# An attention and Fourier-mixing kernel: identity first, block products for every chunk, GpSimd's loads reordered

## Chip, cores and metric

The kernel runs on one core of one Trainium2 chip. Its time is the device time of one execution in microseconds (us); the clock that the throttle granted to TensorE was 1.000 of full speed in the profiled execution.

## What is computed

The input has 4 batches, 8 heads, 768 positions and 64 channels a head. Attention sees the last 96 positions and the first 8 (global) ones, with a bias that falls with the distance at a slope of its own for each head. Its output, 768 x 512 a batch, is mixed by a Fourier transform along both axes (real part), added to itself, normalized, and sent through a two-layer perceptron.

```
scores = q @ k.T / 8 - slope[h] * dist ; outside the band and the first 8 keys: -1e9
x = softmax(scores) @ v                      # heads side by side: (4, 768, 512)
u = x + real(fft(fft(x, axis=1), axis=2))
un = (u - mean(u)) / sqrt(var(u) + 1e-6)
out = u + relu(un @ w_ch1) @ w_ch2           # 512 -> 2048 -> 512
```

## The kernel before

**Units and lists.** All work is cut into units. TensorE's units have a letter and a number: A is attention, M is mixing, H is the first layer of the perceptron and G the second one. A small operation on another engine is named after the unit that created it (A1.0, H9.0) or is T.n if it belongs to no unit of TensorE. The table `ORDER` holds, for each of the five engines (TensorE PE, ScalarE ACT, VectorE DVE, GpSimd POOL, SyncE SP), the list of names in the order in which this engine issues them. Each engine runs its list in order; which engine makes a small operation follows from the list in which its name stands. The numbers of the class `Plan` (`LAT`, `SLOW`, costs in `later`) are a model of the chip; they decide in which of several free PSUM banks a unit works, and in which order the program is emitted, while the order on each engine comes from the lists.

**Attention.** For batches 0 and 1 q and k are loaded by GpSimd's queue (T.11 to T.14, T.19, T.20 for batch 0; T.28 to T.33 for batch 1), with a cast to float16 on the way, all but the first pair of heads: that pair comes by SyncE's and ScalarE's queues (reads T.0, T.2, T.4, T.6, casts T.1, T.3, T.5, T.7). TensorE turns q and k with the identity matrix (`trans`: A0, A1, A5, A6, A15 in batch 0, A25, A26, A30, A34 in batch 1), the turned pair is copied out of PSUM, and the keys of the inner tiles are copied once more into `kB` (the key swap, line 685). A score unit (A2 to A4 and so on) adds the distance bias on TensorE, with the scaled identity and the distance table `dist` (T.9), and ScalarE takes the exponential. The `av` units multiply by v; VectorE divides the result (line 836) into X. v is loaded by T.15 to T.18, T.21 to T.24 (batch 0) and T.58 to T.61 (batch 1), and its inner tiles are copied into `vB` (T.66 to T.69, T.85 to T.88). Batches 2 and 3 are turned by DMA on SP's queue and use the distance table `dist_k` (T.35) by a multiplication instead.

**Mixing.** X is folded (VectorE f1 to f4, g1, g2: T.70 to T.83 for batch 0, T.93 to T.98 for batch 1; partly M0 and M1 on TensorE). The y units (M2, M3, M9, M10 in batch 0; M15, M16, M18, M19 in batch 1) multiply by the table t1 (T.26), the u units (M7, M8, M13, M17) by t2 (T.27); M4 to M6 spread X by a permutation (T.25). For batches 1 to 3 X goes to memory and comes back in rows (T.91 reads it for batch 1). Each batch has three chunks of 256 rows, 12 in all. M11, M12 and M14 turn the normalized chunks 0 to 2, later ones are turned by DMA.

**Perceptron.** H units 8c to 8c+7 make the hidden layer of chunk c. They need the weight pieces of `w_ch1` (T.54 to T.57); unit H(8c+j) needs piece j/2. The second layer has two forms. For chunks below `CS` (0 and 1) `pg_unit` makes it plainly: two halves of 128 rows, each of four units of four matmuls of 512 columns (line 1372), so G0 to G15. Other chunks use block products (`s_sums`, `pg_units`): the product of 2 x 2 blocks is made by 7 products of blocks instead of 8, each of eight matmuls of 256 columns (line 1486), in five units a chunk, six in the last. They need four sums of blocks of the hidden layer (s1 to s4, lines 1450 to 1463, 128 x 1024 each) and four blocks of sums of the weights (`w2_sums`, T.259 to T.262), of which one is written over a part of `w_ch2` itself, so that the last plain product has to be through (`pgdone`). The pieces of `w_ch2` are loaded by T.62 to T.65.

What a unit of GpSimd's load queue waits for is also the eighth load before it, as at most eight are under way:

```
if p[9]:
    t = max(t, (self.lanes[p[9] - 1] if p[9] > 0 else self.soft[-p[9] - 1])[0])
```

Of the kernel before, what the change touches and what calls it, by code (L numbers as in the profile page):

```python
# [14 lines left out]
P = 128  # L15


class Ring(str):

    k = 0  # L20
# [4 lines left out]
class Plan:  # L25
# [11 lines left out]
    LAT = {"ACT": 0.14, "DVE": 0.12, "POOL": 0.08}  # L37
# [84 lines left out]
    def op_go(self, eng, name, start):  # L122
# [6 lines left out]
        if eng == "POOL":  # L129
            self.ports.append((start, end, 1 if dma else 0 if outs and outs[0][0] in ("vB", "kB") else 2))  # L130
# [21 lines left out]

    SHARED = {"kB": 1, "vB": 1, "sid": 1, "f1": 0, "f2": 0, "f3": 0, "z": 0, "g0": 0, "w": 0, "s": 0, "w2a": 0, "w2t": 0, "ex": 0}
# [3 lines left out]
    def beside(self, start, cost, kind):  # L157

        left, t = cost, start
        names = self.todo["POOL"]  # L160
        ports = self.ports[-3:]
        if names:
            s = self.op_start("POOL", names[-1])
            if s is not None:
                p = self.made[names[-1]]
                ports = ports + [(max(s, start), max(s, start) + p[0]["POOL"][0], 1 if p[7] else 0 if p[3] and p[3][0][0] in ("vB", "kB") else 2)]
        for a, b, dma in ports:
            if b <= t:
                continue
            if a > t:  # L170
                if a - t >= left:
                    break
                left -= a - t
                t = a
            rate = self.SLOW[kind][dma]
            if (b - t) * rate >= left:
                return t + left / rate - start
            left -= (b - t) * rate
            t = b
        return t + left - start  # L180
# [40 lines left out]
    def unit_start(self, unit):  # L221
# [7 lines left out]
        if not there:  # L229
# [22 lines left out]
        ),  # L252
        "ACT": (
# [9 lines left out]
        ),  # L263
        "DVE": (
# [11 lines left out]
        ),  # L276
        "POOL": (
# [5 lines left out]
        ),  # L283
        "SP": (
            "T.6 T.0 T.9 T.136 T.35 T.127 T.133 T.128 G7.1 T.134 T.91 G3.1 T.10 T.137 T.130 T.100 T.131 T.101 T.102 T.176 T.182 T.177 T.34 T.185 T.183 "
            "T.140 T.205 T.212 T.206 T.186 T.211 T.149 T.179 T.180 T.150 T.151 T.229 T.189 T.228 T.223 T.222 T.198 T.199 T.200 T.240 T.239 T.245 T.246 "
            "T.256 T.258 T.257 "
# [56 lines left out]
def act(n):  # L344
    return 0.1 + n / 1180.0


def dve(n):
    return 0.13 + n / 960.0
# [6 lines left out]
def pool(n):  # L356
    return 0.16 + n / 1080.0


@with_exitstack  # L360
def kernel(
# [25 lines left out]
    CS = 2  # L387
# [132 lines left out]
    def load_v(b, hp):  # L520
# [7 lines left out]
        if b == 1:  # L528
            for t in range(2 - hp % 2 * 2):
# [3 lines left out]
                swq(four, 1.08, [], [("v", b, hp, t), ("v", b, hp + 1, t)], (1536, 0.93))  # L533
# [172 lines left out]
    def score(b, hp, g):  # L706
# [3 lines left out]
        def run(start, ring):  # L710
# [37 lines left out]
            e = pl.pe((0.45, 0.45, 0.34)[g] if pem else 0.24, start, "64x64" if pem else "64x32")  # L748
# [61 lines left out]
    def av(b, hp):  # L810
# [28 lines left out]
        def part(start, ring, x, k):  # L839
# [15 lines left out]
            pl.later([("DVE", 0.17 + 0.03 * m + m * dve(384), lambda: norm(po, k))], free(*XT[b]), e,  # L855
# [10 lines left out]
    def bounce(b):  # L866
# [26 lines left out]
        pl.later([("POOL", 1.1, rg)], xw + [("xr", b), ("c", "back")], 0.0, [("xg", b)], dma=(128, 4.94), rank=0)  # L893

    def fold_s(b):
# [3 lines left out]
        for n, (c0, cw) in enumerate(parts):  # L899
# [43 lines left out]
            pl.later([("DVE", (4 if b else 2) * dve2(cw), f3)], [("f2", b, n)], 0.0, [("f3", b, n)])  # L943
# [844 lines left out]
```

## Time and profile before

| | |
|---|---|
| median of 3 runs | 248.52 us (247.92 to 248.96) |
| profiled execution | 248.1 us |
| its span, first to last instruction | 246.3 us |
| TensorE busy | 230.6 us (94%) |
| VectorE, ScalarE, GpSimd busy | 193.6, 138.6, 114.1 us |
| read from memory, written | 31.48 MB, 8.65 MB |

Busy times are unions of instruction times on an engine; a matmul's time includes its way through the pipeline, so the price of one in a row of many is the distance of the starts. The two views used most are the timeline (start, length, engine, line, operation, tiles, how many, and in brackets the idle time ahead of it and what ended it) and the stretches (for each stretch its length, then busy time and count of TensorE, its weight loads, VectorE, ScalarE, GpSimd, the granted clock, the share of DMA and GB/s).

### The profile page before, as it was taken

The page shows a single profiled execution, that of the slowest core. Times are in us where ns is not written, and L with a number is a line of the kernel's source. Part 1 is how long each engine was busy: PE and PEld are TensorE (multiplying, and loading weights), DVE is VectorE, ACT ScalarE, POOL GpSimd, SP SyncE. Part 2 cuts the span into 40 slices and gives each one's busy share as a digit, 9 for nine tenths or more (in the row PEclk, how much of TensorE's full clock was granted, in tenths as well). Part 3 has the DMA queues.
Part 4 walks back from the last instruction along what each step waited for, and adds up shares of the span by engine and source line. Part 5 has one row for each costly group of instructions (what it writes and reads, how often), then busy time and mean ns, then how long its engine had stood idle before and what let it go on. Part 6 is the DMA issues. An engine that isn't in the chain of part 4 may idle for free.

```text
span 246.3 us, 7605 instructions
## 1 busy us (share of the span) xinstructions
PE 230.6 (94%) x3251; PEld 191.2 (78%) x3251; DVE 193.6 (79%) x420; ACT 138.6 (56%) x226; POOL 114.1 (46%) x162
## 2 busy tenths in 40 slices
PE   7497896999999998999999999999999999999994
PEld 2375774788668567888988888898889898888883
DVE  2389995879974669999999699899998756746483
ACT  2289687874747458677447788464443761434200
POOL 8699985978391018999139046700210230011020
PEclk9999999999999999999999999999999999999999
DMA  7999999999999999999999989221380240040212
GB/s 178 171 163 141 157 223 148 201 189 201 125 133 168 211 181 204 111 139 114 220 208 266 136 110 148 50 23 22 133 296 4 43 130 0 0 130 1 89 65 106
DMA packets 96082, 32.89 MB, mean 134 GB/s; under 512 B 84304, under 2 KB 92624, under 8 KB 96048
## 3 DMA queue, kind: packets, MB, share of 16 engines
q0 software_dynamic: 66176, 17.06, 72.7%
q1 hardware_dynamic: 26560, 12.56, 25.8%
q10 hardware_dynamic: 3312, 2.79, 3.9%
q8 instruction: 25, 0.41, 0.7%
q14 instruction: 9, 0.07, 0.1%
HBM read 31.48 MB, written 8.65 MB: 163 GB/s over the span
## 4 chain that ended last, share of the span: by engine, by line
PE 49%; DMA 21%; DVE 15%; ACT 4%; POOL 4%; SPq 3%; issue 2%; ACTq 0%; DVEq 0%; POOLq 0%
PE ph L1341 21%; PE pgD L1486 12%; PE pgA L1486 9%; DMA v<-in_v_dram 6%; DMA t<-t1m 4%; DMA ident<-idm 3%; SPq L633 3%; DMA out_dram<-u 3%; PE pav L824 2%; ACT ex L768 2%; DMA unT<-un 2%; POOL qk L554 2%; DMA xr<-xd 2%; DVE tt L836 2%; DMA qk<-in_q_dram 2%
## 5 line engine op out<-in xcount | busy, mean ns | idle before, releaser
L1341 PE MATMUL ph<-unT,w 128*128 128x256 f16 x768 | 94.4, 273 | 1.4 <-DMA unT<-un 0.7
L1341 PEld LDWEIGHTS <-w 128*128 128x128 f16 x768 | 73.7, 98 | 13.2 <-issue 1.2
L1346 ACT ACTIVATE hT<-ph 128x512 f16<-128x512 f32 x73 | 42.9, 596 | 55.1 <-PE ph L1341 53.1
L1486 PEld LDWEIGHTS <-hT 128*128 128x128 f16 x320 | 31.0, 98 | 4.3 <-issue 0.4
L1287 POOL TENSOR_SCALAR sm<-sm 128x2 f32<-128x2 f32 x12 | 3.5, 291 | 58.7 <-ACT un L1280 58.3
L765 ACT ACTIVATE er<-sc 128x1024 f16<-128x1024 f32 (+1 forms) x24 | 22.3, 951 | 11.6 <-PE sc L739 8.0
L1347 DVE TENSOR_SCALAR hT<-ph 128x512 f16<-128x512 f32 x23 | 15.7, 687 | 12.6 <-PE ph L1341 12.6
L768 ACT ACTIVATE ex<-sc 128x1024 f16<-128x1024 f32 (+1 forms) x24 | 21.6, 955 | 5.7 <-PE sc L745 5.6
L1504 DVE SCALAR_TENSOR_TENSOR u<-pgA,sm,u 128x256 f32<-128x256 f32 (+1 forms) x30 | 16.9, 568 | 5.6 <-PE pgA L1486 5.1
L1504 DVE SCALAR_TENSOR_TENSOR u<-pgD,sm,u 128x512 f32<-128x512 f32 (+1 forms) x21 | 15.1, 720 | 3.2 <-PE pgD L1486 3.0
L1357 POOL DMA_INDIRECT out_dram<-u,back x4 | 4.6, 1146 | 27.8 <-DVE rev L1142 16.3
L889 POOL DMA_INDIRECT xr<-xd,back x3 | 4.6, 1525 | 26.1 <-PE sc L739 16.6
L1120 ACT ACTIVATE zy<-py 128x1024 f16<-128x1024 f32 (+1 forms) x13 | 11.1, 857 | 8.8 <-PE py L1107 6.1
L1372 PE MATMUL pg<-w,hT 128*128 128x512 f16 x64 | 16.0, 380 | 0.0
L780 DVE TENSOR_TENSOR ex<-er,mk 128x1024 f16<-128x1024 f16 (+1 forms) x24 | 15.1, 645 | 0.7 <-ACT er L765 0.7
L1280 ACT ACTIVATE un<-un 128x512 f16<-128x512 f16 x24 | 15.0, 625 | 1.1 <-DMA unT<-un 1.1
L1271 ACT ACTIVATE un<-u,sm 128x512 f16<-128x512 f32 x19 | 13.1, 717 | 2.4 <-DVE sm L1238 1.0
L554 POOL DMA_DIRECT2D qk<-in_k_dram x16 | 13.7, 901 | 1.1 <-DMA w<-in_moe_w_ch_dram 0.7
L824 PEld LDWEIGHTS <-ex 128*128 128x128 f16 x352 | 12.6, 97 | 2.0 <-issue 1.2
L824 PE MATMUL pav<-v,ex 128*128 128x65 f16 x224 | 13.1, 193 | 0.6 <-DVE x L836 0.5
L554 POOL DMA_DIRECT2D qk<-in_q_dram x16 | 13.6, 868 | 0.0
L836 DVE TENSOR_TENSOR x<-pav,rc 128x384 f16<-128x384 f32 x24 | 12.6, 554 | 0.6
(168 smaller groups left out, 489.3 us busy)
## 6 DMA issues: line engine op xcount, KB each, us to landing
w<-in_moe_w_ch_dram POOLq DMA_DIRECT2D x8, 512.0 KB, 13.5
out_dram<-u SPq DMA_DIRECT2D x15, 256.0 KB, 2.4
v<-in_v_dram POOLq DMA_DIRECT2D x12, 192.0 KB, 7.6
qk<-in_k_dram POOLq DMA_DIRECT2D x16, 96.0 KB, 6.8
qk<-in_q_dram POOLq DMA_DIRECT2D x16, 96.0 KB, 5.3
xr<-xd SPq DMA_DIRECT2D x3, 512.0 KB, 4.7
xd<-x ACTq DMA_DIRECT2D x2, 768.0 KB, 5.6
v<-in_v_dram POOLq DMA_DIRECT2D x8, 96.0 KB, 5.4
```

The lines of the kernel that those rows point to most:

```text
L554: nc.gpsimd.dma_start(qk16[n][:, w, :, h], src[b, h0 + h].rearrange("(i m) d -> m i d", m=P))
L765: A(mine(), cut(pa), AF.Exp, 0.0, 0.125)
L768: A(cut(expst[hp][:, :, g * 512:g * 512 + (384 if g == 2 else 512)]), cut(pa), AF.Exp, 0.0, 0.125)
L780: VT(o, mine(), m, op=ALU.mult)
L824: nc.tensor.matmul(o[:, s * 65:(s + 1) * 65], lhsT, w, start=(a == 0), stop=(a == len(ops) - 1), skip_group_check=True)
L836: VT(X[b][:, 3 * (k.start + h):3 * (k.start + h) + 3, 2 * hp * Dh:(2 * hp + 2) * Dh].rearrange("p y (h d) -> p y h d", d=Dh), pv[:, h, :, ...
L1341: nc.tensor.matmul(ph[:, a * CH:(a + 1) * CH].rearrange("p (x m) -> p x m", x=2), W1[0][:, d, jb * P:(jb + 1) * P], UNT[c][:, :, d, :], st ...
L1346: pl.later([("ACT", act(512), lambda: A(dst, ph, AF.Relu)), ("DVE", dve(512), lambda: V.tensor_scalar_max(dst, ph, 0.0))], [], e, [("h", c ...
L1347: ("DVE", dve(512), lambda: V.tensor_scalar_max(dst, ph, 0.0))],
L1372: nc.tensor.matmul(pg, HT[c][:, jb, t * P:(t + 1) * P], W2[0][:, jb, :], start=(jb == 0), stop=(jb == NJ - 1))
L1486: nc.tensor.matmul(o, lhs(j), rhs(j), start=(first and j == 0), stop=(j == NK - 1), skip_group_check=True)
L1504: V.scalar_tensor_tensor(o, x, r(t), acc, op0=ALU.mult, op1=ALU.add)
```

## The change

It has three parts, and the lists of all engines are written anew around them.

1. ScalarE's queue issues the identity (T.8) first, then its two reads of q and k (T.2, T.4), then the distance table (T.9, before on SP's queue), and after two casts `dist_k` (T.35, before on SP's queue). ScalarE now casts both parts of k, VectorE both parts of q.
2. `CS` is 0: chunks 0 and 1 also use block products. The G units are numbered anew: chunk c has G5c to G5c+4, the last G55 to G60. The block sums of chunk 0 are T.201 to T.204, of chunk 11 T.263 to T.266, the sums of weights T.270 to T.273. They wait no longer for plain products, and X of batch 1 lies in X's own buffer and not in that of the first loads. A block sum of chunk 3 and later may be made by GpSimd, and 13 of the 48 sums stand on GpSimd's list.
3. GpSimd's loads come in another order. In particular q and k of the fourth pair of heads come second, and t1 (T.26) comes behind t2 (T.27), two loads of v of batch 1 and a piece of `w_ch1`, and ahead of a piece of `w_ch2` (T.65).

Beside that some costs of the model are changed. Of the key swaps of batches 0 and 1 four move from GpSimd to VectorE (A1.0, A15.0, A6.0, A30.0) and one the other way (A5.0).

```diff
-    LAT = {"ACT": 0.14, "DVE": 0.12, "POOL": 0.08}
+    LAT = {"ACT": 0.18, "DVE": 0.12, "POOL": 0.08}
...
         "PE": (
-            "A0 A1 A5 A3 A4 A2 A8 A9 A15 A10 A11 A7 A6 A20 A18 A19 A14 A13 A12 A16 A30 A21 A17 A22 A23 A24 A37 A36 M0 A34 A25 M1 A35 M4 A28 A38 A26 M5 M2 "
-            "A39 A29 M3 M9 A32 M7 A33 A40 M8 M10 A31 M6 A27 M11 M13 A44 H2 H7 A43 H4 H3 M12 A42 H0 H1 A41 H12 G4 H13 H11 G0 H6 H5 M14 G1 G5 G6 H15 G7 H14 "
+            "A0 A1 A5 A4 A3 A15 A2 A20 A19 A18 A9 A8 A7 A6 A10 A11 A16 A12 A13 A14 A17 A30 A21 A22 A23 A24 A25 M1 A34 A26 M0 A36 A35 A38 A40 M4 A29 A28 "
+            "A39 M5 M2 M3 M9 A32 M7 A33 M8 A37 M10 M6 A27 A44 M11 A43 M13 A31 H1 H4 A42 A41 H2 H0 M12 H3 H5 H7 H13 H6 H15 H10 H9 H14 M19 M15 H11 G0 H12 "
+            "M14 M18 H8 M16 G1 G2 M17 G3 G4 G5 H16 H19 G6 A47 H17 G7 A46 H23 H21 G9 H20 A53 A51 H18 H22 G8 A55 A45 G10 H24 A54 A56 H30 G11 A50 A52 H27 "
...
+            "H64 G39 G40 H74 H78 G41 H72 H79 G42 H75 H73 G43 H76 G44 H77 H85 M32 H84 G45 H80 H82 G46 H86 H81 G47 H87 G49 H83 G48 G50 H90 H94 G51 H95 H92 "
+            "G52 H93 H88 G54 H91 H89 G53 G55 G56 G57 G58 G59 G60 "
...
         "ACT": (
-            "T.2 T.4 T.8 T.3 T.5 A1.2 A3.0 A4.0 A2.0 A8.0 A9.0 A7.0 A20.0 A18.0 A19.0 A13.0 A12.0 A14.0 A30.1 A37.0 A36.0 T.72 M0.0 T.77 M0.1 A25.1 M1.0 "
+            "T.8 T.2 T.4 T.9 T.5 T.7 T.35 A1.1 A3.0 A5.1 A2.0 A4.0 A20.0 A19.0 A9.0 A8.0 A7.0 A18.0 A12.0 A13.0 A14.0 A25.1 T.77 M1.0 M1.1 A26.1 M0.0 "
...
         "DVE": (
-            "T.7 T.1 T.49 T.51 A1.1 A5.1 A5.0 T.52 T.66 T.50 A15.1 A11.0 A10.0 A6.1 T.70 T.53 T.68 T.71 A16.0 T.69 A17.0 A22.0 A21.0 T.75 T.73 T.76 A23.0 "
+            "T.49 T.50 T.1 T.3 T.52 A1.2 T.51 A1.0 A15.1 A15.0 T.66 T.53 T.68 A6.1 A6.0 A11.0 A10.0 T.70 A16.0 A30.1 A17.0 A23.0 A24.0 T.75 T.71 T.76 "
...
+            "T.85 M13.2 A42.0 A41.0 T.93 T.94 T.95 T.96 T.201 T.97 T.272 T.98 T.270 T.273 T.271 G0.0 T.202 T.204 G1.0 G2.0 T.203 G3.0 G4.0 T.207 M17.0 "
...
         "POOL": (
-            "T.12 T.11 T.20 T.15 T.16 T.19 T.13 T.14 T.36 T.22 A1.0 T.21 T.18 T.17 T.30 T.31 T.23 A15.0 T.24 T.33 A6.0 T.28 T.67 T.32 T.29 A30.0 T.25 "
-            "T.65 T.26 T.27 T.61 T.60 T.59 A34.0 A25.0 T.56 T.57 T.55 T.58 T.54 T.111 A26.0 T.88 T.118 T.62 T.84 T.64 T.87 T.63 T.121 T.86 M7.8 T.119 "
+            "T.11 T.12 T.19 T.20 T.14 T.15 T.16 T.18 T.13 T.17 T.21 T.22 T.36 T.31 T.30 A5.0 T.24 T.23 T.28 T.29 T.25 T.32 T.33 T.67 T.69 T.27 T.61 T.55 "
+            "T.60 T.26 T.65 T.54 A25.0 T.59 A34.0 T.56 T.58 A26.0 T.62 T.87 T.118 T.84 T.106 T.88 T.111 T.57 T.86 T.116 T.63 T.104 T.64 T.105 T.120 T.108 "
...
+            "T.173 M20.5 T.228 T.148 T.235 T.236 T.238 T.241 T.190 M23.11 M26.5 T.197 T.243 T.246 M29.5 T.245 T.249 T.252 T.254 M29.11 T.259 M32.5 T.266 "
+            "T.262 "
...
         "SP": (
-            "T.6 T.0 T.9 T.136 T.35 T.127 T.133 T.128 G7.1 T.134 T.91 G3.1 T.10 T.137 T.130 T.100 T.131 T.101 T.102 T.176 T.182 T.177 T.34 T.185 T.183 "
+            "T.6 T.0 T.10 T.91 T.130 T.127 T.136 T.133 T.128 T.131 T.137 T.206 T.205 T.134 T.100 T.101 T.185 T.176 T.34 T.186 T.177 T.102 T.216 T.217 "
...
-    CS = 2
+    CS = 0
...
+        def slow(fn):
+            return [("POOL", pool2(NK * P), lambda: fn(nc.gpsimd))] if c > 2 else []
...
-        pl.later([("DVE", us, s1)], hs + sfree(0), 0.0, [("s", c, 1)], rank=1)
+        pl.later([("DVE", us, s1)] + slow(s1), hs + sfree(0), 0.0, [("s", c, 1)], rank=1)
...
-        pl.later(ways if soon else ways[:1], needs, 0.0, [tok], lat=1.0 if soon else 3.2, dma=us)
+        pl.later(ways if soon or tok == ("dk",) else ways[:1], needs, 0.0, [tok], lat=1.0 if soon else 3.2, dma=us)
```

More of the change, by code (lines that the diff above doesn't have):

```diff
@@ L129, in op_go @@
         if eng == "POOL":
-            self.ports.append((start, end, 1 if dma else 0 if outs and outs[0][0] in ("vB", "kB") else 2))
+            self.ports.append((start, end, 1 if dma else 0 if outs and outs[0][0] in ("vB", "kB", "ts", "w1s", "s") else 2))
         if dma:
@@ L165, in beside @@
                 p = self.made[names[-1]]
-                ports = ports + [(max(s, start), max(s, start) + p[0]["POOL"][0], 1 if p[7] else 0 if p[3] and p[3][0][0] in ("vB", "kB") else 2)]
+                ports = ports + [(max(s, start), max(s, start) + p[0]["POOL"][0], 1 if p[7] else 0 if p[3] and p[3][0][0] in ("vB", "kB", "ts", "w1s", "s") else 2)]
         for a, b, dma in ports:
@@ L854, in part @@
             m = k.stop - k.start
-            pl.later([("DVE", 0.17 + 0.03 * m + m * dve(384), lambda: norm(po, k))], free(*XT[b]), e,
+            pl.later([("DVE", 0.08 + 0.03 * m + m * dve(384), lambda: norm(po, k))], free(*XT[b]), e,
                      [("x", b, hp, z) for z in range(k.start, k.stop)], CD(b, ring), ring=ring, rank=RA(b))
@@ L892, in bounce @@
         pl.later([("SP", 0.38, rd)], xw + free("xr", b), 0.0, [("xr", b)], lat=2.0, dma=(128, 10.4))
-        pl.later([("POOL", 1.1, rg)], xw + [("xr", b), ("c", "back")], 0.0, [("xg", b)], dma=(128, 4.94), rank=0)
+        pl.later([("POOL", 1.6, rg)], xw + [("xr", b), ("c", "back")], 0.0, [("xg", b)], dma=(128, 4.94), rank=0)
     def fold_s(b):
@@ L942, in fold_s @@
             pl.later([("DVE", 2 * dve2(2 * cw) + 0.6 * (b + n == 0), f2)], [("f1", b, n)] + free("ww", IW(b, n)), 0.0, [("f2", b, n)])
-            pl.later([("DVE", (4 if b else 2) * dve2(cw), f3)], [("f2", b, n)], 0.0, [("f3", b, n)])
+            pl.later([("DVE", (3.45 if b else 2) * dve2(cw), f3)], [("f2", b, n)], 0.0, [("f3", b, n)])
             if b == 0:
@@ L1144, in r0 @@
             Y[(b, 0, 3, "r")], Y[(b, 3, 3, "r")] = rev[:, 0], rev[:, 1]
-        pl.later([("POOL", 0.8, lambda: r0(nc.gpsimd.tensor_copy)), ("DVE", 0.3, lambda: r0(V.tensor_copy))], [("y", b, 0, 3), ("y", b, 3, 3)] + free("rev0", b), 0.0,
+        pl.later([("POOL", 1.1, lambda: r0(nc.gpsimd.tensor_copy)), ("DVE", 0.3, lambda: r0(V.tensor_copy))], [("y", b, 0, 3), ("y", b, 3, 3)] + free("rev0", b), 0.0,
                  [("y", b, 0, 3, "r"), ("y", b, 3, 3, "r")], [("free", "zy", 2 * b + 1)])
@@ L1274, in centre @@
         for a in range(2):
-            pl.later([("ACT", 0.62, lambda a=a: un("ACT", a)), ("DVE", 1.3 if c < 2 else 0.38, lambda a=a: un("DVE", a))],
+            pl.later([("ACT", 0.62, lambda a=a: un("ACT", a)), ("DVE", 1.3 if c < 2 else 0.55, lambda a=a: un("DVE", a))],
                      [("u", c, a)] + free("un", c), 0.0, [("un", c, a)])
@@ L1288, in rstd @@
             nc.gpsimd.tensor_tensor(r, r, mhalf, op=ALU.pow)
-        pl.later([("POOL", 0.82, rstd)], [("ss", c, 0), ("ss", c, 1)], 0.0, [("rstd", c)], rank=2)
+        pl.later([("POOL", 1.25, rstd)], [("ss", c, 0), ("ss", c, 1)], 0.0, [("rstd", c)], rank=2)
     def nt_dma(c):
@@ L1359, in st @@
                                          in_=UT[c].rearrange("p r d -> p (r d)"), in_offset=None)
-        pl.later([("POOL", 1.1, st)], needs, 0.0, [], [("free", "u", c + pl.U0)] * 2, dma=(128, 11.25), rank=0)
+        pl.later([("POOL", 1.25, st)], needs, 0.0, [], [("free", "u", c + pl.U0)] * 2, dma=(128, 11.25), rank=0)
     def pg_unit(c, t, part):
@@ L1447, in new, with s1, s3, s2 @@
             return SX[c, i]
-        def s1():
-            VT(new(0), block(1, 0), block(1, 1), op=ALU.add)
-        def s3():
-            VT(block(1, 0), block(0, 0), block(1, 0), op=ALU.subtract)
-        def s2():
-            VT(new(1), SX[c, 0], block(0, 0), op=ALU.subtract)
-        def s4():
+        def s1(on=V):
+            on.tensor_tensor(new(0), block(1, 0), block(1, 1), op=ALU.add)
+        def s3(on=V):
+            on.tensor_tensor(block(1, 0), block(0, 0), block(1, 0), op=ALU.subtract)
+        def s2(on=V):
+            on.tensor_tensor(new(1), SX[c, 0], block(0, 0), op=ALU.subtract)
+        def s4(on=V):
             if lean:
                 SX[c, 2] = SX[c, 1]
-                VT(SX[c, 2], block(0, 1), SX[c, 1], op=ALU.subtract)
+                on.tensor_tensor(SX[c, 2], block(0, 1), SX[c, 1], op=ALU.subtract)
             else:
-                VT(new(2), block(0, 1), SX[c, 1], op=ALU.subtract)
+                on.tensor_tensor(new(2), block(0, 1), SX[c, 1], op=ALU.subtract)
         us = dve2(NK * P)
+        def slow(fn):
+            return [("POOL", pool2(NK * P), lambda: fn(nc.gpsimd))] if c > 2 else []
         def sfree(i):
@@ L1471, in s_sums @@
         k = 3 * (c - LATE)
[L1472 to L1475 removed]
+        pl.later([("DVE", us, s1)] + slow(s1), hs + sfree(0), 0.0, [("s", c, 1)], rank=1)
+        pl.later([("DVE", us, s2)] + slow(s2), [("s", c, 1)] + sfree(1), 0.0, [("s", c, 2)], [] if lean else [("free", "sx", k)], rank=1)
+        pl.later([("DVE", us, s4)] + slow(s4), [("s", c, 2)] + ([("p6", c)] if lean else sfree(2)), 0.0, [("s", c, 4)], [] if lean else [("free", "sx", k + 1)], rank=1)
+        pl.later([("DVE", us, s3)] + slow(s3), [("s", c, 1)], 0.0, [("s", c, 3)], rank=1)
     def pg_units(c):
```

26 lines of the change are left out of this document (13 added, 13 removed), and 49 rows, old and new, of the table ORDER.

## The prediction

> **What bounds the kernel now.** I read the page first (shares, slices), then three stretches, then TensorE's waits, then single stretches of the timeline.
>
> ```profile
> PE 230.6 (94%) x3251; PEld 191.2 (78%) x3251; DVE 193.6 (79%) x420; ACT 138.6 (56%) x226; POOL 114.1 (46%) x162
> PE   7497896999999998999999999999999999999994
> DMA  7999999999999999999999989221380240040212
> ```
> ```profile
> 0.00:43.00 43.00, 32.92 (x737) 24.35 (x737) 29.55 (x74) 27.98 (x36) 35.25 (x56) 1.00 1.76 169
> 43.00:60.00 17.00, 16.36 (x357) 13.98 (x355) 14.62 (x37) 11.61 (x18) 15.09 (x25) 1.00 1.43 198
> 60.00:243.00 183.00, 181.30 (x2162) 152.89 (x2160) 149.21 (x310) 98.98 (x172) 63.78 (x82) 1.00 0.84 120
> ```
> The first number behind the comma is PE's busy time. From 60 to 243 us PE stands idle for 1.7 of 183 us, so there the time is the sum of the matmuls, whatever VectorE or GpSimd do. Of the 12.4 us that PE is idle up to 243, 10.1 lie before 43 us. There DMA is full, and PE waits for it and for small steps:
> ```profile
> PE pt L654 <- DMA ident<-idm: 2.3, 1, 2.3
> PE sc L745 <- POOL mk L686: 1.8, 2, 1.1
> PE py L1107 <- issue: 1.5, 1, 1.5
> PE pz L1645 <- DVE eg L1640: 1.4, 1, 1.4
> PE py L1107 <- DMA t<-t1m: 0.8, 1, 0.8
> PE ph L1341 <- DMA w<-in_moe_w_ch_dram: 0.6, 1, 0.6
> ```
> So a change pays by fewer matmuls, or by less waiting before 60 us. The sum is made against the profiled run: 248.1 us, of which the span is 246.3; the median of the runs is 248.52, 0.4 above, which I add at the end.
>
> **Products of chunks 0 and 1.** They are 16 groups of four 512-column matmuls; they become 14 products of eight 256-column ones.
> ```profile
> 60.01 1.03 PE L1372 MATMUL pg<-w,hT 128*128 128x512 f16 x4
> 60.88 1.91 PE L1341 MATMUL ph<-unT,w 128*128 128x256 f16 x16
> ```
> ```profile
> 144.74 0.87 PE pgA L1486 x8
> 145.61 0.67 PE pav L824 x22
> ```
> The distance between starts is the price, as matmuls overlap: 0.87 us for a group of four, and 0.87 us for eight of 256 columns. So 16 x 0.87 = 13.9 becomes 14 x 0.87 = 12.2: **-1.7 us**, in a stretch where PE is the bound. It brings eight block sums of about 0.7 us and larger additions to VectorE, but 13 sums of chunks 3 to 11 go to GpSimd; VectorE has 34 idle us of 183 after 60 us, so this costs nothing in sum.
>
> **The 13 sums on GpSimd.** No such operation is in the trace. A GpSimd copy of 512 columns takes 0.63 us and one of 128 takes 0.32 (below), so 1024 columns with one input are about 1.0 us, and with two at most twice that if each input costs alike; I take 2.0, the upper end, as two operands are read, and 0 as the price on PE. In the new order each sum has PE work between its source and its user: for chunk 9's first sum H85, M32, H84, G45, H80, H82, about 5.2 us at 0.87 each; for the last chunk's s3, four products, 3.5 us. Cover is gone only if a sum takes over 3.5 us. What GpSimd's sums do to VectorE is seen here:
> ```profile
> 18.97 0.35 DVE L968 TENSOR_TENSOR eA<-x 128x384 f16<-128x384 f16 x1
> 19.23 1.21 DVE L969 TENSOR_TENSOR eA<-x 128x384 f16<-128x384 f16 x1
> ```
> ```profile
> 19.59 0.63 POOL L685 COPY mk<-qkT 128x512 f16<-128x512 f16 x1
> 20.28 0.32 POOL L686 COPY mk<-qkT 128x128 f16<-128x128 f16 x1
> ```
> An addition and a subtraction of the same size on VectorE take 0.35 and 1.21 us; the second lies beside GpSimd's copies and loses 0.9 us. If 13 x 2.0 us on GpSimd slow half of what VectorE does beside them, that is 13 us of VectorE, of the 34 that it has idle. The Trainium skill (SBUF — State Buffer, "Who interferes with whom") says that a VectorE operation with two SBUF inputs and a GpSimd operation that reads SBUF exclude each other for the whole instruction. By that rule the row of 1.21 us is one that stood still, and the trace agrees. As an estimate by it, 13 sums hold VectorE for up to 26 us instead of 13; that still fits into the 34, so the sum stays, and the rest of it is rival 4.
>
> **The start.** The identity is now first on ScalarE's queue, the distance table and dist_k last.
> ```profile
> 1.26 0.53 ACTq L570 DMA_DIRECT2D u<-in_k_dram  x1
> 1.82 0.51 ACTq L1610 DMA_DIRECT2D ident<-idm  x1
> 7.18 0.52 ACT L599 ACTIVATE hT<-u 128x384 f16<-128x384 f32 x1 [2.59 <-DMA u<-in_k_dram]
> 8.68 1.31 PE L654 MATMUL pt<-ident,hT 128*64 128x128 f16 x24 [2.32 <-DMA ident<-idm]
> ```
> PE's first transposes could have begun at 7.7 us, behind the cast of k, but the identity came at 8.6. Now that cast is the last; k is issued 0.5 us later, and no longer shares the first queue time with the distance table, which goes the other way by about as much. So PE starts at 7.3 to 8.3, I take 7.8: 0.9 us earlier. The key swap moves from GpSimd to VectorE, behind one more identity scaling: no gain there. But 0.9 us at 8 us is worth something only if nothing later on the way is later, and here one thing is.
>
> **GpSimd's loads.** The table t1 comes from GpSimd's queue behind other loads, and the first y product (M2) needs it.
> ```profile
> 24.29 1.03 POOL L585 DMA_DIRECT2D tt<-in_k_dram  x1
> 27.09 0.74 POOL L1678 DMA_DIRECT2D w<-in_moe_w_ch_dram  x1
> 28.38 0.57 POOL L1634 DMA_DIRECT2D t<-t2m  x1
> 28.92 2.93 POOL L531 DMA_DIRECT2D v<-in_v_dram  x3
> ```
> ```profile
> tt<-in_k_dram POOLq DMA_DIRECT2D x1, 384.0 KB, 6.3
> w<-in_moe_w_ch_dram POOLq DMA_DIRECT2D x1, 512.0 KB, 8.8
> t<-t2m POOLq DMA_DIRECT2D x1, 384.0 KB, 11.6
> v<-in_v_dram POOLq DMA_DIRECT2D x1, 192.0 KB, 12.3
> ```
> ```profile
> 27.83 10.04 DMA t<-t1m
> ```
> ```profile
> 38.01 1.03 PE L1107 MATMUL py<-t,ww 128*128 128x256 f16 x8 [0.78 <-DMA t<-t1m]
> 51.40 1.92 PE L1341 MATMUL ph<-unT,w 128*128 128x256 f16 x16 [0.57 <-DMA w<-in_moe_w_ch_dram]
> ```
> Issue plus time to landing: the last load of q and k (T.29) lands at 30.6, the permutation and a weight piece at 35.9, t1 at 37.9, t2 at 40.0, the first v at 41.2. Each comes out in order, so the queue is full: a step is 5.3, 2.0, 2.1, 1.3 us. In the new order t1 stands behind the same loads of q and k, the permutation and one weight piece, but also behind t2 (2.1) and two v loads (1.3 each): 4.7 us later. Against it, four key swaps (0.95 us each) leave this stretch of GpSimd and one comes in, and what copies are left stand behind the loads of q and k, so the queue is fed earlier: 0 to 2.9 us. The table dist_k, 160 KB, is added early at about 0.9 us (t1's 384 KB in 2.0). So t1 lands between 40.6 and 43.5 if the permutation and a weight piece take 5.3 us again, and between 38.7 and 41.6 if they go at t1's rate (656 KB in 3.4). I take 40.8, a little to the early side, since GpSimd no longer stops for a copy before these loads. VectorE and ScalarE allow M2 at about 39 to 40 by the order of their lists, so the table is the last.
> PE then starts M2 at 40.9 instead of 38.0, but with more done: three scores are moved ahead of M2 and one behind it, 1.0 us. From M2 to the first H unit it was 13.4 us, 2.1 of it waiting (1.5 issue, 0.6 weights); the waits mostly go, since M3 and M9 follow at once; the work is 11.3 less three scores, plus one, plus A43: about 10.95. So H1 starts at 51.85 with A43 (0.65 us) done besides: **-0.2 us** (from -2.3 to +2.5 by the ends for t1).
>
> **Behind it.** On SP's queue the read of batch 1's fold rows (T.91) moves ahead of the transposes of batch 2.
> ```profile
> SPq L633 <- DMA qk<-in_q_dram: 70.6, 3, 54.2
> ```
> Those wait for their loads for 54 us as it is, so a read that is due at about 60 us costs them nothing; were batch 1's attention later than these loads, they would wait for it. H6 and H7 need the weight piece T.57, now issued behind three loads of batch 2; A42 needs a value copy of GpSimd behind it: +0.3. G1 needs the weight sums, which were not needed before chunk 2.
> ```profile
> 61.52 0.96 DVE L909 TENSOR_TENSOR eA<-tt 128x1536 f16<-128x1536 f16 x1
> 71.20 0.74 DVE L1383 SCALAR_TENSOR_TENSOR u<-pg,sm,u 128x512 f32<-128x512 f32 x1
> ```
> ```profile
> L1427 DVE TENSOR_TENSOR tt<-w 128x1024 f16<-128x1024 f16 x2 | 1.5, 729 | 0.1
> ```
> On VectorE stand between A41 and G1: its division (1.3), the fold (61.5 to 71.2 less two strangers of 0.8: 8.9), one block sum (0.7), eight weight sums (8 x 0.7 = 5.6), 16.5 us. On PE 14 H units (12.2), G0, M12, M14 and four y units stand there, about 17. A tie: +0.5 (0 to 2.5). Queued behind the waiting G1 on PE is everything, as PE runs in order.
> The later waits:
> ```profile
> 96.67 1.91 PE L1341 MATMUL ph<-unT,w 128*128 128x256 f16 x16 [0.65 <-DMA unT<-un]
> ```
> Batch 1's fold starts some 3 us earlier, so this one should shrink: -0.3 (-1 to +1).
>
> Sum: -1.7 - 0.2 + 0.3 + 0.5 - 0.3 = -1.4, so 246.7, and on the scale of the median **247.1 us**. Its own range is 245.9 to 248.3.
>
> **Rivals.** (1) *The table t1 is later still, and the weights with it*: t1 at 42.7 (1.9 later) and T.57 0.8 later: 249.8. For it: DMA is full from 2 us on, so putting 0.77 MB ahead is paid unless the feed had gaps. Against: GpSimd has an idle gap and four copies less. It decides from t1 at about 42. (2) *The early gains stay*: t1 at 39, M2 bound by ScalarE at 39.7 (-1.2), nothing lost behind it (-0.8): 245.1. For it: the start is 0.9 us earlier. Against: in-order DMA. (3) *The weight sums come late*: VectorE's fold is slowed by GpSimd's copies as in the row of 1.21 us, G1 waits 2 us: the 1.7 is given back, 248.6, no change. (4) *GpSimd's sums stop VectorE, and this reaches PE*: each of the 13 delays a product by 0.2 us: 249.7; against it stands the 34 us of idle VectorE. The rule above would give this if the stops fell on the last sums ahead of a product. (5) That the block products don't take place is excluded by the order: PE's list is six G units shorter (16 quarter sums become 10 units).
>
> **How the numbers follow.** Forecast 0.42, rivals 0.24, 0.14, 0.14, 0.06. A measurement of this kernel tells about 0.5%, 1.24 us, from no change. Two thirds of the forecast and all of rival 2 lie below 247.3: faster 0.42 x 0.7 + 0.14 = 0.44. The rest of the forecast, nearly all of rival 3 and a tenth of rival 1 lie within: 0.27. Slower: 0.29. The range reaches from a little below rival 2 to a little above rival 1: 244.4 to 250.4, which leaves out the ends of t1.
>
> **What would show it.** Right: the wait for the identity is gone, the first transposes stand at 7.3 to 8.3; the first y product waits for t1 at about 41; no 512-column pg is left, and PE's second products are 1.7 us shorter; a GpSimd sum takes 1 to 2.5 us; PE is idle under 2 us after 75. Wrong: t1 lands before 39 or after 42.5; a wait of over 2 us at G1 for the weight sums; waits for GpSimd's sums among PE's waits; first transposes not before 8.5.

## The result, and the profile after

The changed kernel takes 250.99 us (median of 4 runs, 250.19 to 251.60), the kernel before 248.22 (median of 4, 247.36 to 248.96): a ratio of 1.0111, 95% interval 1.0062 to 1.0159. That is slower by 1.1%, outside the range and on the other side of no change. Of the executions below, two of e4 (252.89 and 253.15 us), three of e8 (252.22 to 253.99), one of e12 (257.84) and four of the kernel before ran over 1.5% longer than the fastest of their kernel; the medians leave them out, while e4's ratio counts its two. The profiled execution took 250.55 us, its span 248.7. Its page, engines and granted clock:

```profile
PE 234.0 (94%) x3299; PEld 198.8 (80%) x3299; DVE 194.5 (78%) x411; ACT 145.6 (59%) x242; POOL 139.6 (56%) x169
PEclk9857999999999999999999999999999999999999
```

The three stretches of the prediction (length, busy time and count of TensorE first):

```profile
0.00:43.00 43.00, 34.88 (x717) 25.78 (x718) 27.27 (x74) 25.76 (x32) 36.60 (x55) 0.88 1.61 180
43.00:60.00 17.00, 16.06 (x320) 13.21 (x318) 15.02 (x35) 14.18 (x24) 14.25 (x23) 1.00 1.53 167
60.00:243.00 183.00, 181.28 (x2252) 158.45 (x2251) 150.49 (x301) 105.62 (x187) 88.71 (x93) 1.00 0.82 117
```

In the third stretch TensorE is as busy as before (181.28 against 181.30), but its last product ends at 244.78 us instead of 242.70. Up to these ends it is idle 1.72 us from 60 us on, and was idle 1.40 before, and it has 183.06 us of work instead of 181.30, though the products of chunks 0 and 1 became 1.7 us cheaper. So some 3.5 us of other work was left over from the first 60 us; 24 matmuls of the hidden layer (2.6 us) and 32 transposes (0.4) are counted in it. The granted clock of 0.88 in the first stretch is a half clock from 11 to 21 us. TensorE's waits, the longest and those that are named below:

```profile
PE pt L660 <- ACT hT L605: 2.8, 1, 2.8
...
PE sc L751 <- DVE mk L692: 1.2, 3, 0.5
...
PE py L1113 <- DVE ww L1085: 0.5, 1, 0.5
...
PE pgD L1495 <- DVE tt L1434: 0.3, 1, 0.3
```

The wait for the identity (2.3 us) is gone, and in its place TensorE waits 2.8 us for the casts of k. Neither t1 nor a weight piece is waited for. The wait for the weight sums (`tt`, line 1434) is 0.3 us, which looks harmless. The chain that ended last says otherwise. First its shares before, then after:

```profile
PE 49%; DMA 21%; DVE 15%; ACT 4%; POOL 4%; SPq 3%; issue 2%; ACTq 0%; DVEq 0%; POOLq 0%
```
```profile
PE 62%; DVE 25%; ACT 3%; DMA 3%; issue 3%; POOL 2%; ACTq 0%; POOLq 0%
```

VectorE's part grew from 15 to 25%, and one piece of the chain after is VectorE alone for 18 us (start, length, what):

```profile
57.07 0.68 PE pav L830 x22
...
60.30 0.96 DVE eA L915
...
67.90 0.55 DVE ww L1072
68.45 0.60 DVE misc L1428
...
74.90 0.70 DVE tt L1434
75.60 0.04 issue
75.64 1.36 PE pgD L1495 x11
```

From the last two attention products of batch 1 (A42 and A41) on VectorE divides, folds (60.30), makes chunk 0's first block sum and the eight weight sums, with nothing between, up to 75.60; G1, the first product that reads a weight sum, starts 0.04 us later. Its first division had waited for TensorE's A42:

```profile
57.78 0.23 DVE L840 RECIPROCAL rc<-pav 128x12 f32<-128x12 f32 x1 [0.31 <-PE pav L830]
```

What TensorE has left at 75 us is seen in the stretch from 75 us to the end, taken for one tile at a time: before, the hidden layer, the wide products, the A and D products, and y; then after, the hidden layer, the A and D products, and y.

```profile
75.00:246.30 171.30, 79.66 (x648) 1.00 0.75 118
75.00:246.30 171.30, 8.07 (x32) 1.00 0.75 118
75.00:246.30 171.30, 31.08 (x240) 1.00 0.75 118
75.00:246.30 171.30, 38.36 (x320) 1.00 0.75 118
75.00:246.30 171.30, 9.04 (x68) 1.00 0.75 118
```
```profile
75.00:248.70 173.70, 78.30 (x640) 1.00 0.74 113
75.00:248.70 173.70, 36.29 (x280) 1.00 0.74 113
75.00:248.70 173.70, 46.00 (x384) 1.00 0.74 113
75.00:248.70 173.70, 6.63 (x51) 1.00 0.74 113
```

Before, half of the products of chunks 0 and 1 are done by then, since wide products need no sum: 32 are left, 7.0 us at 0.87 for four. After, 664 less the 560 of the other ten chunks are left: 104, 11.3 us at 0.87 for eight. Against that stand 8 hidden-layer and 17 y products more done (2.7 us). So at 75 us TensorE is 11.3 - 7.0 - 2.7 = 1.6 us behind, of the 2.1 at the end; 0.3 us more of waiting behind 75 us, the wait at G1 among it, is most of the rest.

### The profile page after: what moved, and what is told of

It is laid out like the page before. It is cut to its first block, busy times and chain, and to the rows that moved or that the text cites. A ratio compares the mean times of both kernels' runs of the same rounds, so it can differ in the third digit from the quotient of the medians.

```text
span 248.7 us, 7723 instructions
## 1 busy us (share of the span) xinstructions
PE 234.0 (94%) x3299; PEld 198.8 (80%) x3299; DVE 194.5 (78%) x411; ACT 145.6 (59%) x242; POOL 139.6 (56%) x169
## 4 chain that ended last, share of the span: by engine, by line
PE 62%; DVE 25%; ACT 3%; DMA 3%; issue 3%; POOL 2%; ACTq 0%; POOLq 0%
PE ph L1347 24%; PE pgD L1495 14%; PE pgA L1495 10%; DVE x L842 4%; PE pu L1200 3%; DMA u<-in_k_dram 3%; PE sc L745 2%; DVE u L1513 2%; PE pav L830 2%; PE py L1113 2%; PE sc L737 2%; PE pt L660 2%; PE sc L751 1%; DVE qkT L684 1%; DVE ww L1085 1%
## 5 line engine op out<-in xcount | busy, mean ns | idle before, releaser
L1352 ACT ACTIVATE hT<-ph 128x512 f16<-128x512 f32 x80 | 46.9, 598 | 56.1 <-PE ph L1347 51.9
L1495 PEld LDWEIGHTS <-hT 128*128 128x128 f16 x384 | 37.1, 98 | 5.1 <-issue 0.5
L1513 DVE SCALAR_TENSOR_TENSOR u<-pgA,sm,u 128x256 f32<-128x256 f32 (+1 forms) x36 | 20.5, 568 | 8.2 <-PE pgA L1495 7.5
L1513 DVE SCALAR_TENSOR_TENSOR u<-pgD,sm,u 128x512 f32<-128x512 f32 (+1 forms) x25 | 18.1, 724 | 9.0 <-PE pgD L1495 7.9
L786 DVE TENSOR_TENSOR ex<-er,mk 128x1024 f16<-128x1024 f16 (+1 forms) x24 | 17.5, 739 | 1.0 <-ACT er L771 0.9
L842 DVE TENSOR_TENSOR x<-pav,rc 128x384 f16<-128x384 f32 x32 | 16.7, 554 | 0.7
L1353 DVE TENSOR_SCALAR hT<-ph 128x512 f16<-128x512 f32 x16 | 11.0, 686 | 8.0 <-PE ph L1347 7.7
L1456 POOL TENSOR_TENSOR eg<-hT 128x1024 f16<-128x1024 f16 x3 | 6.4, 2136 | 18.7 <-ACT hT L1352 17.4
L1495 PEld LDWEIGHTS <-sb 128*128 128x128 f16 x128 | 12.4, 98 | 2.4 <-issue 0.9
L737 PE MATMUL sc<-misc 64*64 64x512 f16 (+1 forms) x96 | 12.1, 450 | 2.0 <-ACT ex L774 0.8
```

What stands on the lines that cost most here:

```text
L737: nc.tensor.matmul(o, sid[r, 2 * hp + s, r], m, start=True, stop=False, skip_group_check=True, tile_position=(64 * s, 64 * t))
L786: VT(o, mine(), m, op=ALU.mult)
L842: VT(X[b][:, 3 * (k.start + h):3 * (k.start + h) + 3, 2 * hp * Dh:(2 * hp + 2) * Dh].rearrange("p y (h d) -> p y h d", d=Dh), pv[:, h, :, ...
L1352: pl.later([("ACT", act(512), lambda: A(dst, ph, AF.Relu)), ("DVE", dve(512), lambda: V.tensor_scalar_max(dst, ph, 0.0))], [], e, [("h", c ...
L1495: nc.tensor.matmul(o, lhs(j), rhs(j), start=(first and j == 0), stop=(j == NK - 1), skip_group_check=True)
L1513: V.scalar_tensor_tensor(o, x, r(t), acc, op0=ALU.mult, op1=ALU.add)
```

## The experiments

All ran with interleaved runs of the kernel before, whose medians were 248.2 (first four), 248.3 (next three), 248.0 (e8 to e10), 248.9 (e11) and 248.0 (e12). In brackets stand the ratio to them and its 95% interval. Medians less than about 1.2 us apart are not told apart; the clock times in the traces are sharper. "Lists" are the orders of the five engines.

**Halves and starts.** The first theories were that the loss arises before the first hidden-layer units (E), or in the later half (L); and within the first, in the start (S) or in the order behind it (O).

```
e1   before's lists up to TensorE's unit A41, then the changed kernel's (CS = 0)
e2   the changed kernel's lists up to A41, then before's (CS = 2)
e3   changed kernel; ACT: - T.8 T.2 T.4 T.9 T.5 T.7 T.35   + T.2 T.4 T.8 T.5 T.7 (T.35 behind A14.0)
                     SP:  - T.6 T.0 T.10                   + T.6 T.0 T.9 T.10
e4   kernel before;  ACT: - T.2 T.4 T.8                    + T.8 T.2 T.4 T.9
                     SP:  - T.6 T.0 T.9                    + T.6 T.0
```

> The changed kernel, but each engine follows the list of the kernel before up to the unit A41 (about 59 us), and the rest of the changed list behind it (block products for all chunks, 13 sums on GpSimd). Theory E (the loss arises before the first hidden-layer units, +3.1 us there, and the products give their 1.7 us back later): 246.5 to 247.5 us, below the kernel before. Theory L (the block products and the sums on GpSimd cost what they save, or more): 248.5 to 250.5 us.

> The other crossing: the changed lists up to A41, behind it the lists of the kernel before (plain products for chunks 0 and 1, all sums on VectorE). Theory E: 251 to 252 us, the loss without the gain, and worse than the changed kernel. Theory L: 248 to 249 us, like the kernel before.

> The changed kernel with the starting loads of the kernel before: ScalarE's queue issues its two reads of q and k first and the identity third, SyncE's queue the distance table third, and dist_k comes after the exponentials of batch 0. Theory S (the identity in front pushes the read of k back by one place, and that is most of the loss): the first transposes begin at about 8.7 us without a stop, the total is 249.0 to 249.8 us. Theory O (the order behind the start, with scores first and the divisions late, is the loss): within 0.5 us of the changed kernel, 250.5 to 251.3 us.

> The kernel before with the new starting loads: identity first, then the reads, then the distance table, all on ScalarE's queue; nothing else is changed. Theory S: the read of k lands at about 8.9 instead of 7.1 us, the first transposes end 0.8 to 1.5 us later, and the total is 249.0 to 250.0 us. Theory O: 248.0 to 248.6 us.

Measured: e1 252.86 us (1.0179, 1.0139 to 1.0219); e2 251.68 (1.011, 1.0054 to 1.0166); e3 250.38 (1.0078, 1.0040 to 1.0116); e4 249.49 (1.0105, 1.0044 to 1.0165). By the medians the new early half costs 3.5 us with the old later half (1.3 to 4.1 by the interval), the new later half 4.7 us with the old early half, and both together only 2.8. Neither E nor L can be the whole, and e1 has the number of neither. In e1 TensorE is as far at 60 us as before (59 hidden-layer products against 56), and then stands:

```profile
PE py L1109 <- DVE ww L1068: 2.4, 1, 2.4
PE ph L1343 <- ACT hT L1348: 1.8, 1, 1.8
```

The first is M19, the first product of batch 1's fold; the second is a copy behind a bounce write (T.89) in ScalarE's queue that waits for a division of VectorE. So an early half that is faster is met by VectorE's fold. The new start alone (e4) costs some 1.3 us in the kernel before, what S foretold, and less than the whole early half; 1.3 us is hardly more than can be told apart. In the changed kernel its removal (e3) brings 0.6 us, less than can be told apart. But e3 does not give the old start back: the reads come as before, and the transposes start at 9.20 us, since q's casts stay on VectorE, behind the scaling of the identity, and TensorE waits 2.7 us for them. So e3 takes back 0.26 of the 0.78 us and does not decide between S and O.

**Where in the early half, and the GpSimd sums.**

```
e5   before's lists up to A19 (24 us), then the changed kernel's
e6   before's lists up to M9 (43 us), then the changed kernel's
e7   changed kernel; POOL: - T.218 T.219 T.235 T.236 T.238 T.241 T.243 T.246 T.249 T.252 T.254 T.259 T.266
                     DVE:  + the same 13
```

> The changed kernel with the queues of before on all five engines up to the end of the score units of the first head pairs (unit A19 on TensorE, about 24 us), and its own queues from there; the same set of units is done at the cut in both orders. Beside the earlier run that put back the loads of the start alone (250.38 us), it puts back the order of the first attention products: the first division in VectorE's queue comes at 16.8 us as before, not at 23.8 us. Theory O (the late divisions of the first 24 us are the loss of the early stage, 3.1 us at the first hidden-layer units, and the block products give back 1.2 of it): 246.5 to 248.0 us, first division before 17.5 us, first hidden-layer matmuls near 51.5 us. Rival M (the order between 24 and 43 us, with the fold, is the loss): 249.5 to 250.5 us, with the hidden layer still past 54 us.

> The changed kernel with the queues of before up to the unit M9 on TensorE (about 43 us, the fold of the first half), and its own queues from there, its block products and GpSimd sums among them. Theory O: no more than 0.5 us beside the run cut at 24 us, 246.5 to 248.0 us. Rival M: here alone the loss goes, 246.5 to 248.0 us, while the cut at 24 us stays at 249.5 to 250.5. Theory L (the later half, with its weight sums and GpSimd sums, costs what the block products save, so that no early order helps): 248.5 us or more in both.

> The changed kernel with its 13 token sums of GpSimd (2.1 us each) put into VectorE's queue, at the places that their planned starts give; nothing else changes. If the sums on GpSimd cost by the lock on the port (VectorE's sum beside one took 1.66 us, alone 0.69) or by lateness, the time falls by 0.5 to 1.0 us, to 250.0 to 250.5; if they are hidden, as the prediction had it, VectorE gets 13 x 0.69 = 9 us more in its queue at 55 of 60 us busy, and the time stays within 0.5 us of 250.99 or grows by up to 2 us, to 253.

Measured: e5 250.29 (1.0084, 1.0054 to 1.0114), e6 252.05 (1.0126, 1.0078 to 1.0173), e7 251.12 (1.0120, 1.0075 to 1.0165). O and M both fall as the whole loss: the old order of the first 24 or 43 us doesn't bring the time back, and both times are those of theory L (no early order helps). e6 has the first y product at 36.9 us, earlier than before, and loses that to a weight piece, since the two load orders don't fit:

```profile
PE ph L1343 <- DMA w<-in_moe_w_ch_dram: 2.9, 1, 2.9
```

e7 stays within 0.2 us of the changed kernel: the sums on GpSimd are neither a cost nor a gain that can be told apart.

**What the later half lacks.** Two theories: TensorE lacks work ahead of the fold, as the wide products that filled it are gone (F), or VectorE's added sums make the wait (V). e10 mirrors e5 on the kernel before.

```
e8   kernel before; PE: the units G4 G0 G1 G5 G6 G7 G2 moved behind M19 and H9; DVE: H9.0 ahead of G7.0
e9   kernel before; - CS = 2   + CS = 1, chunk 1's eight G units replaced by five,
     DVE: the weight sums and chunk 1's block sums behind T.98
e10  the changed kernel's lists up to A11 (24 us), then before's (CS = 2)
```

> The kernel before with one thing moved: its seven whole-width products of chunk 0 that TensorE runs before the first product of the second fold (units G4 G0 G1 G5 G6 G7 G2 before M19, 32 of 128-by-512 matmuls in all with G3) go behind M19; VectorE's queue is as before but for one evacuation; no block product, no weight sum, no GpSimd sum. Theory F (filler: until VectorE ends the second fold near 69 us, TensorE has only attention, hidden-layer units and these products to do; whoever takes the products away gives TensorE a wait for the fold): a wait of 3 to 6 us at the first product of the second fold, near 65 to 70 us, and 251 to 254 us. Theory V (the block products' own sums on VectorE make the wait of the run with the old early half): no wait over 1 us there and 247.5 to 249 us.

> The kernel before with block products for chunk 1 alone: chunk 0 keeps its eight whole-width units where they stood, before and behind M19; chunk 1's eight units become five, VectorE gets the four weight sums 10 us earlier and four token sums (4 x 0.68 us) more. Theory F: with the filler in place the early half is kept and TensorE saves 0.8 us (half of the 1.6 us that the groups of second products show between the kernels), 247.0 to 248.5 us, and no wait over 1 us between 60 and 75 us. Theory V: VectorE's 2.7 us of token sums and the earlier weight sums put a wait of 2 us or more behind 69 us, 249.5 to 251 us.

> The mirror of the run that put back the first 24 us: the kernel before, whole-width products and all, with the changed kernel's queues up to its unit A11 (same set of units at the cut), its own from there. If the first 24 us lose PE time that counts once the later half has no wait to hide it (theory E): 250.0 to 251.5 us, with 1 to 2 us less matmul work done by 60 us than in before. If their loss is taken up before 60 us: 248.0 to 249.0 us.

Measured: e8 250.46 (1.0060, 1.0015 to 1.0105), e9 254.02 (1.0210, 1.0157 to 1.0263), e10 250.47 (1.0080, 1.0043 to 1.0118). In e8 TensorE is idle 2.7 us between 60 and 75:

```profile
60.00:75.00 15.00, 12.30 (x132) 1.00 1.63 131
```

The kernel before is not idle there (15.00 of 15 us), so the wide products do fill that place. But only 0.9 us of the wait stand at the first product of the fold, where F foretold 3 to 6; 1.8 stand at the hidden layer, which waits for its own copies. The time lies between the ranges of F and V. So e8 bears out F in part. e9 has no wait between 60 and 75 us either; behind it one of VectorE's weight sums waits for a transfer out of the buffer that it writes, and TensorE waits for VectorE:

```profile
83.43 0.69 DVE L1424 TENSOR_TENSOR tt<-w 128x1024 f16<-128x1024 f16 x1 [2.78 <-DMA xd<-tt]
```
```profile
87.56 0.77 PE L1483 MATMUL pgD<-tt,hT 128*128 128x256 f16 x4 [2.06 <-DVE tt L1425]
```

So e9 measures the buffer (X of batch 1 lies in `tt` when `CS` isn't 0) and says nothing for or against block products of one chunk. e10 shows 2.5 us (1.1 to 2.9 by the interval) for the first 24 us where TensorE is the bound, as E expected.

**The chain on VectorE.** Theory W: fold and weight sums on VectorE set the start of G1, and the end follows. e11 is to take away TensorE's idle time of e1; e12 adds to VectorE's chain alone.

```
e11  as e1; PE:  - H14 M19 M15 H11 G0 H12 M14 M18 H8 M16   + H14 H11 H12 H8 G0 M14 M19 M15 M18 M16
            ACT: T.89 T.90 behind H6.0; H11.0 H12.0 H8.0 M14.0 ahead of M15.0
e12  changed kernel, in w2_sums, one():
     + for _ in range(3):
           VT(W2T(1)[:, k0], W2[0][:, k1, HC:Dm], W2[0][:, k0, HC:Dm], op=ALU.subtract)
```

> The run with the queues of before up to the unit A41 and the changed kernel's from there (252.86 us; TensorE idle 4.2 us between 60 and 75 us), with two things moved: the hidden-layer units H11 H12 H8, the first product G0 (which reads no weight sum) and the transposes M14 go ahead of M19, the first product of the second fold, so 4.5 us of ready matmuls lie where TensorE waited 2.4 us for the fold; and the two bounce writes T.89 T.90, which stood in ScalarE's queue 2.9 us for a division of VectorE ahead of three evacuations, go behind these. Theory F (only the ready work ahead of M19 is short): no wait over 1 us at M19, TensorE busy 14 of 15 us or more between 60 and 75, 248.0 to 249.5 us. Theory W (VectorE is next: its eight weight sums, 5.6 us behind the fold, end near 76.5 us whatever TensorE does): the wait moves to the first product that reads a weight sum, 2 to 4 us between 72 and 77 us, and 251.0 to 252.5 us.

> The changed kernel with the first weight sum of each half done three times over by VectorE (the same values are written again): four more sums of about 0.6 us each in VectorE's queue behind the second fold, 2.4 us in all; TensorE, ScalarE and GpSimd get nothing more. In the seven kernels with block products for all chunks that have run, TensorE ended 169.0 to 169.1 us after its first product that reads a weight sum, whatever it had done before. Theory W (VectorE's chain of fold and weight sums sets that start): the first such product at 78.0 us in place of 75.6, the end 169.1 us behind it, 253.0 to 253.7 us. Rival P (TensorE's own lateness in the first 60 us sets the end, and VectorE has slack here): 250.8 to 251.7 us.

Measured: e11 251.11 (1.0114, 1.0063 to 1.0165), e12 255.46 (1.0299, 1.0271 to 1.0326). In e11 TensorE has done 70 hidden-layer products by 60 us, 14 more than before and 38 more than after, and still:

```profile
60.00:75.00 15.00, 11.22 (x125) 1.00 1.91 197
```
```profile
75.19 1.03 PE L1491 MATMUL pgD<-tt,hT 128*128 128x256 f16 x8 [1.02 <-DVE tt L1430]
...
243.21 1.04 PE L1491 MATMUL pgD<-w,hT 128*128 128x256 f16 x8
```

All of TensorE's lead is spent in 3.8 idle us up to 75 us, and G1 starts 0.45 us earlier than after. F falls with that; W's time came, and its wait at G1 in part (1.0 us instead of 2 to 4; the rest are waits for copies). In e12 VectorE's six sums take 2.14 us for each three instead of 0.68, 2.9 us more, and TensorE waits 2.9 us at G1:

```profile
70.99 2.14 DVE L1429 TENSOR_TENSOR misc<-w 128x1024 f16<-128x1024 f16 x3
```
```profile
81.14 1.08 PE L1496 MATMUL pgD<-tt,hT 128*128 128x256 f16 x8 [2.90 <-DVE tt L1435]
```

(The profiled execution of e12 took 257.84 us and the other seven 253.56 to 256.10, so only places and waits are read from it.) The median is 4.5 us above the changed kernel's. That excludes P and lies 1.8 us above W's range. The trace shows 2.9 us of the rise as the longer chain. In its one execution two parts more are seen: the chain starts 2.5 us later, as A42 does, and a granted clock of 0.89 from 75 to 90 us, behind the wait, makes the rest 1.6 us longer. How much of that the other seven had isn't shown; the one with a mean clock of 0.999 took 253.56 us, 3.4 more than the changed kernel's execution with the same clock (250.19). The timelines of all eight kernels with `CS = 0`, one execution each, for e3 (252.17 us) the slowest, too (the first two columns: how long VectorE stood waiting for A42's product, and when it began to divide it):

| kernel | wait for A42 | division | weight sums end | G1 starts | TensorE ends | from G1 to the end |
|---|---|---|---|---|---|---|
| changed | 0.31 | 57.78 | 75.59 | 75.64 | 244.78 | 169.1 |
| e1 | none | 58.73 | 76.56 | 77.78 | 246.85 | 169.1 |
| e3 | 1.51 | 59.60 | 77.25 | 77.31 | 246.38 | 169.1 |
| e5 | 0.42 | 57.12 | 74.76 | 74.81 | 243.87 | 169.1 |
| e6 | 3.15 | 58.44 | 76.37 | 76.42 | 245.48 | 169.1 |
| e7 | 0.31 | 57.88 | 75.53 | 75.59 | 244.55 | 169.0 |
| e11 | none | 57.51 | 75.13 | 75.19 | 244.25 | 169.1 |
| e12 | 0.31 | 60.29 | 81.09 | 81.14 | 251.87 | 170.7 |

But for e1, G1 starts 0.05 us behind the last weight sum, and what follows is of one length but for e12. From the division to the last weight sum it is 17.6 to 17.9 us in all but e12 (20.8). So the end hangs on when VectorE begins to divide A42's product. In the six kernels with the changed order from 43 us on or earlier VectorE stands and waits for that product, so TensorE's first half does set the end, through A42 and not through the hidden-layer products that it has done. In e1 and e11, which have the old order up to A41, VectorE's own list sets it: there it had stood 1.7 and 1.0 us for a load of v at 51 us and worked without a stop from then on:

```profile
57.51 0.22 DVE L836 RECIPROCAL rc<-pav 128x12 f32<-128x12 f32 x1
```

So e11's lead of 38 products over the changed kernel moved the division by 0.27 us. And as TensorE's other work and VectorE's chain both start at A42 in the changed kernel and are of nearly one length, its wait at G1 is only 0.3 us. Shown is that lengthening the chain lengthens the time, and that leading TensorE ahead in products that the chain doesn't need doesn't shorten it. No run shortened the chain or brought A42 and A41 forward alone, and none put more ready work ahead of G1, so what these would bring isn't shown; and no version was found that beats the kernel before.

## Why the prediction was wrong

**Products of chunks 0 and 1.** Right: eight 256-column matmuls start 0.87 us apart (75.64 to 76.51 in the timeline), 14 such products replace 16 groups of 0.87. The 1.7 us are saved, but 13 of the 14 products come from G1 on; of the wide products, which need no sum, half had been done by 75 us.

**GpSimd's sums.** Right: 2.0 us was taken for one and 2.1 measured, and nothing on TensorE.

```profile
L1456 POOL TENSOR_TENSOR eg<-hT 128x1024 f16<-128x1024 f16 x3 | 6.4, 2136 | 18.7 <-ACT hT L1352 17.4 <-DVE rc L840 1.3
```
```profile
237.62 2.12 POOL L1459 TENSOR_TENSOR hT<-hT 128x1024 f16<-128x1024 f16 x1 [8.61 <-DVE mk L1456]
```
```profile
238.63 1.66 DVE L1462 TENSOR_TENSOR mk<-mk,hT 128x1024 f16<-128x1024 f16 x1
```

VectorE's sum beside one takes 1.66 us instead of 0.69 and ends 0.55 us after it. That fits the exclusive lock of the Trainium skill (SBUF — State Buffer, "Who interferes with whom"). e7 shows that TensorE doesn't feel it.

**The start.** Wrong, and the first part of the step that failed. It was to bring 0.9 us; TensorE's transposes start at 9.46 instead of 8.68. ScalarE's queue, its first cast and the transposes:

```profile
0.73 0.38 ACTq L1619 DMA_DIRECT2D ident<-idm  x1
...
1.76 0.57 ACTq L576 DMA_DIRECT2D u<-in_k_dram  x1
...
8.88 0.52 ACT L605 ACTIVATE hT<-u 128x384 f16<-128x384 f32 x1 [4.70 <-DMA u<-in_k_dram]
```
```profile
9.46 2.06 PE L660 MATMUL pt<-ident,hT 128*64 128x128 f16 x42 [2.79 <-ACT hT L605]
```

The prediction let k's read cost its 0.5 us of later issue and took the distance table out of the same time; the read, issued 0.5 us later, was cast 1.7 us later (8.88 against 7.18), and in e4 and e10, with the same start, at 8.83 and 8.57. Why the later read takes that much longer isn't shown.

**M2 and H1.** M2 was put at 40.9 us, waiting for t1; it came at 42.88 without waiting for a load. H1 came at 55.15 us, not 51.85:

```profile
42.88 1.95 PE L1113 MATMUL py<-t,ww 128*128 128x256 f16 x16
...
55.15 1.92 PE L1347 MATMUL ph<-unT,w 128*128 128x256 f16 x16
```

The sum's -0.2 us stands for all of this, and the 3.5 us of work left over at 60 us came in its place. The step costed only t1. It left out that TensorE's list puts five more score and transpose units ahead of the first attention product (A10), which VectorE's list waits for: VectorE's first division stood at 24.75 us (16.77 before). That explains little of M2, though: e5 puts this division back to 16.37 us, and M2 comes 1.1 us earlier (41.82); with the old order up to 43 us (e6) it comes at 36.86. So most of M2's delay comes from the lists between 24 and 43 us, and which of their changes makes it isn't shown. The half clock at the start isn't it: e7, with the same lists up to there and a clock of 1.00, has M2 at 42.51 and H1 at 55.26. With the old later half the start alone cost 1.3 us (e4), the first 24 us 2.5 (e10), all up to A41 3.5 (e2).

**G1.** The second step that failed, and the one for which a good early half alone brings no gain (e11: 251.11 us). The lengths were right: 16.5 us on VectorE between A41's division and G1 (16.66 measured, from 58.98), some 17 on TensorE, a wait of 0.5 (0.34 measured). But the prediction compared two lengths and not two clock times. By its own forecast the fold of batch 1 would start 3 us earlier, at 58.5. With the 15.3 us measured from there to the last weight sum (60.30 to 75.60) these end at 73.8; 169.1 us of matmuls behind that end at 242.9, no gain at all. For its sum of -1.4 (an end at 241.3) G1 had to start at 72.2. As the fold came only 1.2 us earlier, behind a late A42, G1 was at 75.64. Rival 3 named the wait for the weight sums with 0.14, but as a fold slowed by GpSimd's copies and a wait of 2 us; it didn't see that the wait can hide in TensorE's own lateness.

**Behind it.** The waits behind 60 us were put at 0.3 + 0.5 - 0.3 = 0.5 us together; TensorE's idle time from 60 us to its last product is 0.3 us more, the wait at G1 included. So the sum came out as -1.7 + 3.5 + 0.3 = 2.1 us in the profiled executions, where -1.4 was forecast.

## What to carry over

Before taking matmuls away from the engine that bounds a stage, ask what those matmuls waited for: work that needs nothing fills the place in front of a long chain on another engine, and a cheaper form that must wait for that chain gives its saving back there. Put the rival chains on one clock, from a row of the profile to the instruction where they meet, not side by side as lengths. And a wait of 0.3 us at such a meeting doesn't say that the other engine is free: look at the chain that ended last, and at what released its first piece. Leading the waiting engine ahead helps only where it does sooner what the other engine waits for.

## What the runs showed of the hardware beside that

Behind some waits of TensorE the granted clock fell to 0.50: for about 3.4 us (an estimate from stretches of 1 us) behind waits of 2.0 us in e5, 2.2 in e8, 2.4 in e1 and 2.9 in e12, and from 11 to 21 us behind the 2.8 us at the start here. In e3, behind a wait of 2.7 us, and in the kernel before, behind 2.3, it stayed at 1.00, and so it did in e11, whose 3.8 idle us lay in waits of at most 1.2. The Trainium skill (TensorE: Matmul & The Clock Gate, Part 1) gives half rate after a free-running window of about 3.4 us of idleness; the half rate is seen here, at shorter waits and not behind each of them.

Three sums of VectorE that write the same place started 0.73 us apart in e12 (2.14 us in all). Sums of the same size that read the result of the one before start 0.72 us apart in the changed kernel (71.38, 72.10, 72.82), and sums that have nothing to do with each other 0.60 (70.78, 71.38).
